# A Fourier filter and a mixture of experts on one core: zero writes and weight loads at other places, shorter row fetches, an earlier pick, an earlier flag

## The chip, the cores and the metric

The kernel runs on one core of one Trainium2 chip. The metric is the time on the device in microseconds (us), from the start of the launch to its end. The kernel before takes 481.42 us, the median of three runs (480.68 to 495.76). The profiled execution shows a span of 480.1 us; all times below that name a moment are counted from the start of this span.

## The reference

Eight sequences of 2496 tokens with 256 channels go through a filter in the frequency domain. Then each token goes to one of eight experts, an expert keeps the 80 tokens with the largest gate, and only kept tokens get a result; all others are zero.

```python
X = np.fft.rfft(x, axis=1)                      # x: 8 x 2496 x 256
y = np.fft.irfft(X * (filt_r + 1j * filt_i), n=2496, axis=1)
x = y.reshape(19968, 256)

logits = x @ w_gate                             # 8 experts
expert_idx = np.argmax(logits, axis=1)
gate_w = softmax(logits)[np.arange(N), expert_idx]
out = np.zeros((N, D))
for e in range(8):
    tok_idx = np.where(expert_idx == e)[0]
    if len(tok_idx) > 80:                       # keep the 80 largest gates
        keep = np.argpartition(-gate_w[tok_idx], 80)[:80]
        tok_idx = tok_idx[keep]
    h = np.maximum(x[tok_idx] @ w1[e], 0.0)     # 256 x 1024
    out[tok_idx] = gate_w[tok_idx, None] * (h @ w2[e])
```

At most 640 of 19,968 rows are not zero. So the kernel transforms back only the picked tokens, and writes the zeros of the output (20 MB) itself.

## The kernel before

It has three stretches.

1. **Steps** (about 24 to 292 us): 80 steps, ten for each of the eight sequences, take the spectrum, multiply it with the filter and turn it. `step(k)` also runs what a plan has put at step k: loads, logits, gating (the candidates' keys), zero writes. After the fifth sequence a first `pick` chooses places among those five.
2. **Groups** (about 298 to 400 us): 40 groups, five for each sequence, fetch for each picked token its row of a table (10 KB), turn it, and multiply it with the sequence's spectrum. Up to 128 tokens of one sequence are one tile. The result of a sequence goes to `y_sel` in device memory. `aside[i]` names what else is issued after group i: spectra (`yb`), zeros, weights, the second pick. The sequences go in the order 0, 1, 3, 4, 2, 5, 6, 7.
3. **Experts** (about 400 to 471 us): the tokens of each expert are gathered from `y_sel` (those of the last sequence come from on-chip memory through a product with a one-hot matrix), and go through the two layers; results are scattered into the output. A flag `bad` says if the quick choice was not exact; then a slow path under `tc.If` does all again. With this input it is not entered.

The parts that the change and the prediction touch, cut:

```python
def put_zeros(n):                       # 26 pieces of 768 KB, on SyncE's DMA queue
    for i in zeros[:n]:
        nc.sync.dma_start(out=out[...], in_=zero_t[...])
    del zeros[:n]

def load_weights(e, pool, tag):         # two DMAs of 1 MB, on SyncE's queue
    w = pool.tile([128, NS, C], F32, ...)
    nc.sync.dma_start(out=w1, in_=moe_w1[e]...)
    nc.sync.dma_start(out=w2, in_=moe_w2[e]...)

# end of pick(): the list of rows for each sequence; lo is -1 where a place is free
nc.vector.tensor_scalar(out=idxb[:, nb0:nb], in0=lo[:, 0:n_b], scalar1=0.0, op0=AL.max)

# plan of the steps (NU = 10 steps a sequence; "put(step, place, what)")
k = NU * 4 + LATE                       # 42
for b0, at0 in ((0, 5), (2, 11)):       # keys of sequences 0,1 and 2,3
    for i, at in enumerate((0, 0, 1, 2, 4, 5)):
        put(k + at0 + at, 2, part(gating, b0, i))
k = NU * NA + LATE                      # 52
put(k + 2, 1, part(logits, 4, 4, 0, 0))
for i, at in enumerate((7, 7, 8, 8, 10, 11)):
    put(k + at, 2, part(gating, 4, i))
for at in (12, 13, 14, 15, 16, 17, 19, 20, 21, 22, 24):
    put(k + at, 0, more_pick)
for at in (2, 3, 3, 4, 4, 5, 5, 6, 7, 8, 10, 12, 14, 16, 18, 20, 22, 24):
    put(NU * 4 + at, 2, part(put_zeros, 1))

def fetch(t):                           # 128 rows of 10 KB, indirect DMA from GpSimd
    gts[t] = pools["mn"[t % 2]].tile([128, NS * 128], F32, ...)
    nc.gpsimd.indirect_dma_start(out=gts[t][:], in_=rows[:, :], in_offset=...idxb[:, b:b + 1])

# the groups
def turn_rows(i):                       # 4 transposes, ScalarE copies; then fetch(t + 2)
    ...
def rows_out(i):                        # 4 products of the token tile with the spectrum
    ...
    if g == NGR - 1:
        nc.scalar.copy(out=yr[:], in_=po)
        if t + 1 < B:
            nc.sync.dma_start(out=y_sel[128 * b:128 * b + 128, :], in_=yr[:])
        else:
            st["yr"] = yr

def gather_slots():                     # issued after group 35
    for e in range(E):
        nc.gpsimd.indirect_dma_start(out=xg[:, e, :], in_=y_sel[:, :], in_offset=...idx1[:, e:e + 1])

for e, i in enumerate((30, 35, 26, 37, 39)):
    aside[i].append(part(load_weights, e, ...))
for i in (2, 4, 5, 24, 27, 29, 31, 33):
    aside[i].append(lambda: put_zeros(1))
for i in range(B * NGR + 1):
    if i < B * NGR: turn_rows(i)
    if i: rows_out(i - 1)
    for f in aside.get(i, ()): f()

# the experts
slots_in(0); slots_last(0); slots_in(1); slots_last(1)   # px: turn the gathered tokens
hT = layer1(0, ...)
for e in range(E):
    if e + 1 < E: hT2 = layer1(e + 1, ...)
    layer2(e, hT, ...)                  # ends in the scatter of expert e
    hT = hT2
    if e + 5 < E: load_weights(e + 5, ...)

n_bad = nc.values_load(bad[0:1, 0:1], min_val=0, max_val=1 << 20)
with tc.If(n_bad > 0), ExitStack() as ictx:
    ...                                 # slow path, not entered
```

Of the kernel before, what the change touches and what calls it, by code (L numbers as in the profile page):

```python
# [90 lines left out]
def kernel(  # L91
# [146 lines left out]
    with ExitStack() as fctx, tc.manual_schedule():  # L238
# [329 lines left out]
        def pick(final):  # L568
# [146 lines left out]
            for k in range(KR):  # L715
# [6 lines left out]
                                           in1=lo[:, 0:n_b], op0=AL.mult, op1=AL.add)  # L722
            nc.vector.tensor_scalar(out=idxb[:, nb0:nb], in0=lo[:, 0:n_b], scalar1=0.0,
                                    scalar2=None, op0=AL.max)

# [161 lines left out]
        def part(f, *a):  # L887
            return lambda: f(*a)
# [22 lines left out]
        for b, at in ((0, 3), (1, 4), (2, 6), (3, 7)):  # L911
            put(k + at, 1, part(logits, b, 0, 0, b % 2))
            put(k + at, 2, part(logits, b, 0, 1, b % 2))
        for b0, at0 in ((0, 5), (2, 11)):
            for i, at in enumerate((0, 0, 1, 2, 4, 5)):
                put(k + at0 + at, 2, part(gating, b0, i))

        k = NU * NA + LATE
        put(k, 2, part(logits_e, 4, 0))
        put(k + 2, 1, part(logits, 4, 4, 0, 0))  # L920
        put(k + 2, 2, part(logits, 4, 4, 1, 0))
        for i, at in enumerate((7, 7, 8, 8, 10, 11)):
            put(k + at, 2, part(gating, 4, i))
        for at in (12, 13, 14, 15, 16, 17, 19, 20, 21, 22, 24):
            put(k + at, 0, more_pick)
        for at in (2, 3, 3, 4, 4, 5, 5, 6, 7, 8, 10, 12, 14, 16, 18, 20, 22, 24):
            put(NU * 4 + at, 2, part(put_zeros, 1))

        gts, wts, pos = {}, {}, {}

        def fetch(t):
            b = ORDER[t]
            gts[t] = pools["mn"[t % 2]].tile([128, NS * 128], F32, name=f"gt_{b}", tag="gt")
            nc.gpsimd.indirect_dma_start(  # L934
                out=gts[t][:], out_offset=None, in_=rows[:, :],
                in_offset=bass.IndirectOffsetOnAxis(ap=idxb[:, b:b + 1], axis=0))

# [5 lines left out]

        put(k + 24, 1, make_room)
        put(k + 24, 1, part(fetch, 0))

# [42 lines left out]
        def rows_out(i):  # L989
            t, g = divmod(i, NGR)  # L990
            b = ORDER[t]
            if g == 0:
                pos[t] = yps.tile([128, 2, 512], F32, name=f"po_{t}", tag="y")
            po = pos[t][:, 0, 0:C]
            for m in range(SG):
                s = SG * g + m
                nc.tensor.matmul(po, lhsT=wts[i][:, m, :], rhs=yk[b][g][:, m, :],  # L997
                                 start=(s == 0), stop=(s == NS - 1))
            if g == NGR - 1:
                yr = pools["n"].tile([128, C], F32, name=f"yr_{t}", tag="yr")  # L1000
                nc.scalar.copy(out=yr[:], in_=po)
                if t + 1 < B:
                    nc.sync.dma_start(out=y_sel[128 * b:128 * b + 128, :], in_=yr[:])
                else:
                    st["yr"] = yr

# [79 lines left out]
        for i, b in ((1, 3), (6, 4), (15, 5), (20, 6)):  # L1086
            aside.setdefault(i, []).append(part(spectrum, b))
        for e, i in enumerate((30, 35, 26, 37, 39)):
            aside.setdefault(i, []).append(part(
                load_weights, e, *((keep_b, "kb") if e < 2 else (keep_a, "ka"))))  # L1090
        for i in (2, 4, 5, 24, 27, 29, 31, 33):
            aside.setdefault(i, []).append(lambda: put_zeros(1))
# [15 lines left out]
        for e in range(E):  # L1108
            if e + 1 < E:
                hT2 = layer1(e + 1, st["xs"][:, :, e + 1, :], pools["f"])  # L1110
            layer2(e, hT, pools["f"])
            hT = hT2
# [37 lines left out]

    n_bad = nc.values_load(bad[0:1, 0:1], min_val=0, max_val=1 << 20)  # L1151
    with tc.If(n_bad > 0), ExitStack() as ictx:

# [453 lines left out]
```

## Time and profile before

| | before |
|---|---|
| time, median of three | 481.42 us |
| span of the profiled execution | 480.1 us |
| TensorE matmul busy | 440.9 us (92%) |
| VectorE / ScalarE / GpSimd busy | 183.0 / 168.7 / 155.3 us |
| bytes moved by DMA | 133.16 MB, mean 277 GB/s |
| mean granted TensorE clock | 0.96 |

The page gives for each engine the busy time, then the span in 40 slices of 12 us: each digit is the busy share of a slice in tenths. The row PEclk is the share of its full clock that TensorE was granted; the row DMA is the busy share of the 16 DMA engines. The timeline lists instructions in order of time: start, duration, engine, line of the kernel, operation, output and inputs, and in brackets how long the engine had been idle and what ended that. PE is TensorE, DVE VectorE, ACT ScalarE, POOL GpSimd, SP SyncE; a q marks what an engine's sequencer does.

### The profile page before, as it was taken

To read this page: it belongs to the slowest core of one execution; us is meant where nothing else is said; L and a number is where in the kernel's file an instruction comes from. 1 tells how busy PE (TensorE), PEld (TensorE's weight loads), DVE (VectorE), ACT (ScalarE), POOL (GpSimd) and SP (SyncE) were. 2 spreads that over 40 slices of the span, in tenths; PEclk is the share of its full clock that TensorE was granted. 3 is DMA by queue.
4 is the path that set the end of the run, shared out by engine and by line. 5 is a ranking of instruction groups with operands and counts; after the bars stand their busy time and mean duration, and the time that the engine had idled before them with its cause. 6 is when DMAs were issued, how large, how long until landed. Compare 5 with 4: busy or idle time off the path is not lost. (4 is left out here: it accounts for less than half of the span.)

```text
span 480.1 us, 7888 instructions
## 1 busy us (share of the span) xinstructions
PE 440.9 (92%) x2933; PEld 374.6 (78%) x2933; DVE 183.0 (38%) x374; ACT 168.7 (35%) x406; POOL 155.3 (32%) x219
## 2 busy tenths in 40 slices
PE   4899989899999999989999789999998997999992
PEld 4899666568788778779989788678887786988881
DVE  2376333225444344255799972242541010100000
ACT  1323534444444543552544323554321230111110
POOL 5023222225455443333566474000036005001101
PEclk9999999999999999989999989999999898799996
DMA  6869899978999999999999509497889999459200
GB/s 222 241 193 274 254 331 338 364 255 263 362 287 328 371 400 398 359 299 342 317 381 387 221 1 374 149 294 313 288 323 390 346 354 351 133 165 298 99 8 20
DMA packets 69440, 133.16 MB, mean 277 GB/s; under 512 B 5452, under 2 KB 51766, under 8 KB 67728
## 3 DMA queue, kind: packets, MB, share of 16 engines
q1 hardware_dynamic: 58838, 91.92, 57.6%
q10 hardware_dynamic: 8074, 28.27, 14.9%
q0 software_dynamic: 2480, 12.37, 7.2%
q8 instruction: 25, 0.41, 0.3%
q14 instruction: 23, 0.19, 0.1%
HBM read 81.56 MB, written 51.07 MB: 276 GB/s over the span
## 5 line engine op out<-in xcount | busy, mean ns | idle before, releaser
L409 DVE TENSOR_TENSOR p<-pb,ft 128x1024 f32<-128x1024 f32 x80 | 97.6, 1222 | 91.5 <-PE pb L404 85.4
L415 POOL TENSOR_TENSOR yt<-p 128x256 f32<-128x256 f32 x80 | 60.2, 753 | 168.0 <-PE py L427 108.2
L427 PEld LDWEIGHTS py<-gi,yt 128*128 128x128 f32 x640 | 83.4, 193 | 21.0 <-issue 11.0
L427 PE MATMUL py<-gi,yt 128*128 128x136 f32 x640 | 90.0, 284 | 6.1 <-POOL yt L417 5.7
L404 PE MATMUL pb<-d_t,t 128*128 128x128 f32 x640 | 89.3, 284 | 2.0 <-ACT t L350 1.9
L404 PEld LDWEIGHTS pb<-d_t,t 128*128 128x128 f32 x640 | 81.5, 199 | 4.6 <-ACT t L350 2.2
L348 PE MATMUL pa<-x,wf_t 128*128 128x512 f32 x128 | 61.1, 605 | 1.8 <-DMA x<-in_x_dram 1.3
L417 POOL TENSOR_TENSOR yt<-p 128x256 f32<-128x256 f32 x80 | 59.1, 739 | 0.0
L350 ACT COPY t<-pa 128x512 f32<-128x512 f32 x64 | 36.7, 587 | 53.5 <-PE pa L348 30.6
L997 PE MATMUL po<-yb,wt 128*128 128x256 f32 x160 | 39.4, 391 | 2.9 <-ACT wt L985 2.9
L985 ACT COPY wt<-pw 128x512 f32<-128x512 f32 x40 | 23.2, 586 | 49.0 <-PE pw L984 43.3
L997 PE MATMUL po<-yk,wt 128*128 128x256 f32 x160 | 37.9, 381 | 1.3 <-ACT wt L985 1.3
L348 PEld LDWEIGHTS pa<-x,wf_t 128*128 128x128 f32 x128 | 22.6, 195 | 20.9 <-issue 16.6
L450 ACT COPY ysp<-py 128x512 f32<-128x512 f32 x40 | 23.4, 585 | 39.8 <-PE py L427 22.5
L450 ACT COPY yk<-py 128x512 f32<-128x512 f32 x40 | 23.5, 587 | 33.3 <-PE py L427 30.2
L997 PEld LDWEIGHTS po<-yb,wt 128*128 128x128 f32 x160 | 29.6, 195 | 6.6 <-ACT wt L985 3.2
L997 PEld LDWEIGHTS po<-yk,wt 128*128 128x128 f32 x160 | 28.9, 190 | 4.9 <-ACT wt L985 1.8
L369 PE MATMUL pn<-wn_t,x 117*128 117x120 f32 x176 | 23.7, 295 | 8.3 <-DMA x<-in_x_dram 8.3
L1053 PEld LDWEIGHTS ph<-xs,w 128*128 128x128 f32 x256 | 30.0, 193 | 0.9 <-issue 0.4
L1053 PE MATMUL ph<-xs,w 128*128 128x80 f32 x256 | 29.6, 275 | 0.0
L369 PEld LDWEIGHTS pn<-wn_t,x 117*128 117x128 f32 x176 | 22.7, 210 | 8.6 <-issue 8.6
L934 POOL DMA_INDIRECT gt<-rows_tbl,idxb x8 | 8.7, 1081 | 62.5 <-PE pw L984 49.9
(184 smaller groups left out, 411.5 us busy)
## 6 DMA issues: line engine op xcount, KB each, us to landing
out_dram<-zero_t SPq DMA_DIRECT2D x26, 768.0 KB
x<-in_x_dram SPq DMA_DIRECT2D x32, 512.0 KB
d<-t ACTq DMA_DIRECT2D x32, 512.0 KB
w<-in_moe_w_dram SPq DMA_DIRECT2D x16, 1024.0 KB
t<-d SPq DMA_DIRECT2D x30, 512.0 KB
yf<-ysp ACTq DMA_DIRECT2D x20, 512.0 KB
yb<-yf SPq DMA_DIRECT2D x4, 2560.0 KB
x<-in_x_dram SPq DMA_DIRECT2D x25, 156.0 KB
```

The lines of the kernel that those rows point to most:

```text
L348: nc.tensor.matmul(out=ps, lhsT=wf_t, rhs=xt[:, 2 * i:2 * i + 2, :], start=True, stop=True)
L350: nc.scalar.copy(out=t1[:, 2 * i:2 * i + 2, :], in_=ps)
L369: nc.tensor.matmul(out=ps[:, j].rearrange("p h s r -> p (h s r)"), lhsT=xt[0:NP1, j, 128 * cb:128 * cb + 128], rhs=wn_t, start=True, stop= ...
L404: nc.tensor.matmul(out=ps[:, i, cb], rhs=d_t[:, s, :], start=True, stop=True, lhsT=st["t2", b, s // SG][:, s % SG, 128 * cb:128 * cb + 128])
L409: nc.vector.tensor_tensor(out=pt, in0=ps[:].rearrange("p s c r q -> p (s c) r q").unsqueeze(1).to_broadcast(shape), in1=ft[:, u].unsqueeze ...
L415: nc.gpsimd.tensor_tensor(out=yt[:, :, 0, :], in0=pt[:, 0, :, 0, :], in1=pt[:, 1, :, 1, :], op=AL.subtract)
L417: nc.gpsimd.tensor_tensor(out=yt[:, :, 1, :], in0=pt[:, 0, :, 1, :], in1=pt[:, 1, :, 0, :], op=AL.add)
L427: nc.tensor.matmul(out=ps[:, i, 136 * cb:136 * cb + 136], rhs=gi[:, cb, :], lhsT=yt[:, 2 * i + cb].rearrange("p r q -> p (r q)"), start=Tr ...
L450: nc.scalar.copy(out=ys[:, m:m + 2, :].rearrange("p i (k c) -> p i k c", k=NDB), in_=ps[:, :, 0:288].rearrange("p i (k c) -> p i k c", k=N ...
L985: nc.scalar.copy(out=wts[i][:], in_=ps[:])
L997: nc.tensor.matmul(po, lhsT=wts[i][:, m, :], rhs=yk[b][g][:, m, :], start=(s == 0), stop=(s == NS - 1))
L1053: nc.tensor.matmul(ph[:, fc // 4, fc % 4, 0:cap], lhsT=w1s[e][:, k, 128 * fc:128 * fc + 128], rhs=xs[:, k, :], start=(k == 0), stop=(k == ...
```

## The change

It has six parts.

1. **Zeros.** 15 instead of 18 of the 26 zero pieces are put in the steps, more of them between steps 62 and 72; the other 11 come after groups 2 to 27, none later. It is meant to put the writes where the DMA engines have room.
2. **Weights.** Those of experts 1, 3 and 4 are issued after the last group (40), not after 35, 37 and 39, so that they do not stand beside the gather of the tokens.
3. **Free places.** A place of a tile that no token has gets a row number beyond the table, so that a bounds check leaves it out of the fetch. The first two sequences keep row 0 in free places, so that both buffers are full once and no place holds undefined data.
4. **Keys and pick.** The keys of sequences 2 and 3 come one step sooner, those of sequence 4 and the first pick two steps sooner, and with them the first fetch.
5. **Last tile.** Its result is written to `y_sel` too, though the gather leaves it out.
6. **Flag.** `bad` is read into the engines' registers ahead of the last expert's second layer, without the check of its bounds, and the code is laid out so that the way past the slow path needs no jump.

```diff
@@ end of pick() @@
-            nc.vector.tensor_scalar(out=idxb[:, nb0:nb], in0=lo[:, 0:n_b], scalar1=0.0,
-                                    scalar2=None, op0=AL.max)
+            if not final:
+                nc.vector.tensor_scalar(out=idxb[:, 0:2], in0=lo[:, 0:2], scalar1=0.0,
+                                        scalar2=None, op0=AL.max)
+            nb1 = nb0 if final else 2
+            free = tl([128, B], F32, "free")
+            nc.vector.tensor_scalar(out=free[:, 0:nb - nb1], in0=lo[:, nb1 - nb0:n_b], scalar1=0.0,
+                                    scalar2=65536.0, op0=AL.is_lt, op1=AL.mult)
+            nc.vector.tensor_tensor(out=idxb[:, nb1:nb], in0=lo[:, nb1 - nb0:n_b],
+                                    in1=free[:, 0:nb - nb1], op=AL.add)
@@ plan of the steps @@
-        for b0, at0 in ((0, 5), (2, 11)):
-            for i, at in enumerate((0, 0, 1, 2, 4, 5)):
-                put(k + at0 + at, 2, part(gating, b0, i))
+        for b0, ats in ((0, (5, 5, 6, 7, 8, 9)), (2, (10, 10, 11, 12, 14, 15))):
+            for i, at in enumerate(ats):
+                put(k + at, 2, part(gating, b0, i))
-        put(k + 2, 1, part(logits, 4, 4, 0, 0))
+        put(k + 1, 1, part(logits, 4, 4, 0, 0))
-        for i, at in enumerate((7, 7, 8, 8, 10, 11)):
+        for i, at in enumerate((5, 5, 6, 6, 8, 9)):
             put(k + at, 2, part(gating, 4, i))
-        for at in (12, 13, 14, 15, 16, 17, 19, 20, 21, 22, 24):
+        for at in (10, 11, 12, 13, 14, 15, 17, 18, 19, 20, 22):
             put(k + at, 0, more_pick)
-        for at in (2, 3, 3, 4, 4, 5, 5, 6, 7, 8, 10, 12, 14, 16, 18, 20, 22, 24):
+        for at in (2, 3, 5, 7, 10, 14, 18, 22, 26, 27, 28, 29, 30, 31, 32):
             put(NU * 4 + at, 2, part(put_zeros, 1))
@@ fetch() @@
-                in_offset=bass.IndirectOffsetOnAxis(ap=idxb[:, b:b + 1], axis=0))
+                in_offset=bass.IndirectOffsetOnAxis(ap=idxb[:, b:b + 1], axis=0),
+                bounds_check=S - 1, oob_is_err=False)
-        put(k + 24, 1, make_room)
-        put(k + 24, 1, part(fetch, 0))
+        put(k + 22, 1, make_room)
+        put(k + 22, 1, part(fetch, 0))
@@ rows_out() @@
-                if t + 1 < B:
-                    nc.sync.dma_start(out=y_sel[128 * b:128 * b + 128, :], in_=yr[:])
-                else:
-                    st["yr"] = yr
+                nc.sync.dma_start(out=y_sel[128 * b:128 * b + 128, :], in_=yr[:])
+                st["yr"] = yr
@@ aside the groups @@
-        for e, i in enumerate((30, 35, 26, 37, 39)):
+        for e, i in ((0, 30), (1, 40), (2, 26), (3, 40), (4, 40)):
-        for i in (2, 4, 5, 24, 27, 29, 31, 33):
+        for i in (2, 3, 4, 5, 6, 13, 14, 17, 21, 24, 27):
@@ the experts @@
             if e + 1 < E:
                 hT2 = layer1(e + 1, st["xs"][:, :, e + 1, :], pools["f"])
+            else:
+                n_bad = nc.values_load(
+                    bad[0:1, 0:1], min_val=0, max_val=1 << 20,
+                    skip_runtime_bounds_check_because="a sum of counts")
             layer2(e, hT, pools["f"])
@@ the flag @@
-    n_bad = nc.values_load(bad[0:1, 0:1], min_val=0, max_val=1 << 20)
-    with tc.If(n_bad > 0), ExitStack() as ictx:
+    with tc.If(n_bad > 0, preferred_fallthrough_block=False), ExitStack() as ictx:
```

## The prediction

> **What bounds the kernel now.** I read the page's slices first, then a table of ten-microsecond stretches, then the timeline of the places where TensorE stands still, then the end.
>
> ```profile
> PE   4899989899999999989999789999998997999992
> ...
> DVE  2376333225444344255799972242541010100000
> ...
> PEclk9999999999999999989999989999999898799996
> DMA  6869899978999999999999509497889999459200
> ```
>
> TensorE is busy nearly everywhere, and DMA too, with a hole at slices 22 and 23 (264 to 288 us). A gain must come from where TensorE stands still or is slowed. The stretches name these places (columns: start and end, length, busy us and instructions of PE, PEld, DVE, ACT and POOL, granted clock, DMA share, GB/s):
>
> ```profile
> 270.00:280.00 10.00, 6.96 (x50) 6.58 (x50) 9.58 (x17) 2.20 (x7) 6.00 (x7) 0.90 0.15 59
> ...
> 360.00:370.00 10.00, 10.00 (x58) 8.76 (x57) 1.43 (x13) 2.23 (x5) 7.59 (x10) 1.00 1.00 399
> 370.00:380.00 10.00, 7.08 (x30) 5.76 (x29) 0.00 (x0) 2.43 (x5) 1.80 (x2) 0.83 1.08 390
> ...
> 390.00:400.00 10.00, 10.00 (x56) 8.77 (x53) 0.00 (x0) 2.66 (x5) 3.38 (x4) 1.00 1.07 386
> 400.00:410.00 10.00, 7.12 (x29) 5.55 (x27) 0.49 (x1) 0.80 (x2) 4.18 (x5) 0.72 1.06 331
> 410.00:420.00 10.00, 10.00 (x65) 9.21 (x65) 0.98 (x2) 0.86 (x2) 0.00 (x0) 0.77 0.31 98
> ```
>
> At 270 VectorE is full (9.58 of 10 us) and TensorE waits for it. At 360 to 380 and 390 to 410 the DMA share is 1.0 or more; TensorE drops to 7.1 us of 10, and then the clock is low too. The timeline of the second place:
>
> ```profile
> 390.34 0.34 SPq L1003 DMA_DIRECT2D y_sel<-yr  x1
> ...
> 391.76 1.89 SPq L230 DMA_DIRECT2D w<-in_moe_w_dram  x1
> ...
> 394.71 5.71 SPq L230 DMA_DIRECT2D w<-in_moe_w_dram  x1
> ...
> 395.70 0.95 POOL L1013 DMA_INDIRECT xg<-y_sel,idx  x1 [21.83 <-DMA y_sel<-yr]
> ...
> 396.68 3.62 PE L997 MATMUL po<-yk,wt 128*128 128x256 f32 x16
> ...
> 401.89 0.64 PE L1024 MATMUL px<-ident,xg 80*128 80x80 f32 x4 [1.59 <-DMA xg<-y_sel,idx]
> ...
> 404.46 0.94 POOL L1013 DMA_INDIRECT xg<-y_sel,idx  x1 [0.30 <-issue]
> ...
> 414.33 5.84 PE L1053 MATMUL ph<-xs,w 128*128 128x80 f32 x50
> ```
>
> The result of the seventh tile is sent at 390.34, but the gather waits until 395.70 for it (5.4 us). The first gathered expert is used at 401.89, 6.2 us after its issue. Between them 6 MB of weights are issued (391 to 401). TensorE has ended the groups at 400.30 (its last `po`, 396.68 + 3.62) and begins the layers at 414.33: 14.0 us for work that is short. The stretch at 360 has one more stall, 5.12 us of ScalarE with no releaser that the profile names, and TensorE stands still 2.92 us behind it:
>
> ```profile
> 372.60 1.07 ACT L985 COPY wt<-pw 128x512 f32<-128x512 f32 x2 [5.12 <-remote]
> ```
>
> The end, for GpSimd (columns: count, ns least/median/most, first and last start):
>
> ```profile
> L1152 POOLq EVENT_SEMAPHORE  x5: 17/42/43, 474.6 to 474.9; - x5
> ...
> L1152 POOLq COMPARE_BRANCH  x1: 53/53/53, 471.7 to 471.7; - x1
> ...
> L1152 POOLq INC_SWDGE_SEM  x1: 980/980/980, 475.0 to 475.0; - x1
> ```
>
> It branches at 471.7, and the next thing that its sequencer does is at 474.6, though the last scatter (issued 471.40) has its last packet at 473.6 in the trace's DMA records. From the last product (470.57) to the end (480.13) are 9.6 us.
>
> [...] the clock is 0.5 from 404.4 to 414.6[...], after the idle time at 400 to 404. [...] a gather of 80 KB takes 6.2 us beside the weights, the scatter of the same size, alone, 2.2 us (471.40 to 473.6). [...] 2.9 us from branch to next action on GpSimd, as much on VectorE (464.8 to 467.7) and ScalarE (471.2 to 474.0).
>
> **The change part by part.** I count from E, the end of the last group's products (400.30 before).
>
> *Weights after the gather (parts 2 and 5).* Nothing but the gather is then in flight from about E-13 on: the weights of expert 0 (issued 380 to 381, 2 MB at some 380 GB/s, 5.5 us) are done by then. The seventh result, issued at E-10.0, should land after about 2.3 us (the scatter's quiet time), and before it took 0.8 us from the landing to the first gather, so the gathers start at E-6.9 and not at E-4.6. They keep their spacing: eight in 8.76 us, so the last is issued at E+1.9 and lands at E+4.2. Experts 0 to 3 (16 products of 0.11 us) and their four of the last tile (1.2 us) fit between E and E+3 with no wait. After the last landing remain four products (0.45 us) and the last tile's four (1.2 us): layers from E+5.8 instead of E+14.0, so 8.2 us less. I take off 0.6 for a chance of one in three that the small gaps still halve the clock[...]. Part 5 I read as a latch: the write of the last tile must wait until the gathers have read `y_sel`, and as the weights stand behind it on SyncE's queue, they wait too. Expert 1's first megabyte is then issued near E+4.8; that of expert 5 (issued 425.23, nothing else in flight) had its last packet about 4.4 us later, so E+9.2. Layer one of expert 1 starts at E+5.8 + 3.5 (32 products of 0.11) = E+9.3. This is a tie; 0.3 us for it. Left: **7.3 us**.
>
> *Flag (part 6).* The load is 0.5 us on each sequencer, hidden: TensorE's queue runs about 3.4 us ahead there (its branch waits 3418 ns), ScalarE and GpSimd are idle. Without the jump GpSimd meets the last landing at about 473.75 and not 475.0: **1.25 us**. The 0.98 us of semaphore work and a drain of 3.26 us after it stay.
>
> *Zeros (part 1) and free places (part 3).* About 80 of 128 places are taken (640 tokens over eight sequences), so six fetches bring some 48 x 10 KB less: 2.9 MB of 133, or 7.7 us of DMA time at 380 GB/s, but each fetch had slack: that of the eighth tile was issued at 372.9 and used at 387.6. Their direct worth is nil. The zeros after groups 29, 31 and 33 (0.77 MB each, 2 us) go away from the stretch at 360 to 380, where 4.6 us are lost: 2.9 of idle time[...]. If a full DMA is the cause, this goes; if not, not. I give it 0.4 of 4.6: **1.8 us**. The zeros at steps 66 to 72 go into the hole of DMA, 256 to 275 us. The eight zero pieces that held SyncE's queue from 168 to 195 become five; TensorE has no idle time there.
>
> *Keys and pick (part 4).* It moves the full VectorE, and does not thin it: some 17 us of pick against 0.6 us of room in each step (1.82 us a step, 1.22 for the filter product). Sequence 4's first keys now fall on the step of the last ones of 2 and 3, and `idxb` costs two more operations (0.2 to 0.4 us each). The first fetch, issued at 286.9, was in time at 297.7 anyway. I set 0, from +0.5 to -1.
>
> Sum: 7.3 + 1.25 + 1.8 = 10.4 us off, **481.4 to 471.0 us**.
>
> **The rivals.** (a) *The weights become the bound.* They start some 14 us later; if the latch lets go late or two megabytes must land first, TensorE waits 2 to 4 us ahead of layer one of expert 1: 474 to 475. For it: the tie above. Against it: only the first of the two megabytes is needed there, and later experts have 14 us more. (b) *The gather stays slow.* If the write of the last tile does not wait, the weights meet gathers five to eight, which take 6.2 us again: last landing near E+8, layers from E+9.6 or later with a half clock: 475 to 476. For it: nothing in the profile shows the latch. Against: gathers one to four are quiet even so. (c) *The gain is larger.* With the stall at 370 gone for good and less in the way of the steps at 200 to 230, 466 to 468. (d) *VectorE's crowding costs more*, as keys of three sequences touch: 1 to 2 us.
>
> **Range and chances.** From 466.5 (c) to 477 (a, b and d in part). Over 2% faster means under 471.8, which is close by my number: 0.54; within 2%: 0.44; slower: 0.02, as nothing is added on the path but the tie.
>
> **What would show it.** Right: the wait of the gather for `y_sel` ends about 3 us after the seventh result is issued; gathers are used at once; no clock of 0.72 at the start of the experts; layers begin near E+6; GpSimd's semaphore work starts within 0.2 us of the last landing. Wrong: weights issued before the last gather lands (b), TensorE idle ahead of the second expert (a), or the stall of 5 us near the sixth tile still there, which takes the 1.8 away.

## The result and the profile after

| | before | after |
|---|---|---|
| time, median (four executions of each on one chip) | 481.05 us (480.55 to 495.76) | 478.85 us (473.77 to 483.32) |
| ratio after/before, 95% interval | | 0.9864 (0.9828 to 0.9899) |
| span of the profiled execution | 480.1 us | 481.0 us |
| TensorE matmul busy | 440.9 us | 438.5 us |
| bytes moved by DMA | 133.16 MB | 131.20 MB |
| mean granted TensorE clock of that execution | 0.960 | 0.963 |

The change makes the kernel 1.4% faster, where 2.2% (481.4 to 471.0 us) was predicted. The medians here are of all executions, the ratios only of those within 1.5% of the fastest of the same kernel, so 0.9864 is not 478.85 / 481.05. By the ratio the kernel after stands at 474.5 us (0.9864 x 481.05), inside the predicted range; the median of all four lies 1.85 us above that range. Measured a second time, unchanged (after_again below), the ratio was 0.995: the two measurements put the gain at 0.5 and 1.4%. Executions of one and the same kernel differ by up to 3.7% (before, in the set of after_again), and the clock that TensorE was granted differs with them: after_again took 474.91 us at a mean clock of 0.977 and 488.62 us at 0.949. So most of what follows counts from E, the end of the last group's products, inside one execution.

Slices of the page of after, in the order of those of before:

```profile
PE   4889989799999999989989699989999799899990
...
DVE  2466323135444344355699972143532010000000
...
PEclk9999989999999999987999999999999999599996
DMA  6768889987999998297689988199999943989000
```

The hole of DMA at slices 22 and 23 is full (9 and 8): that is where the zeros of steps 66 to 72 (issued up to 273.8) and the first fetch (283.6, before 286.9) went; lower ones now stand at slices 16 (2) and 25 (1, before 4). The loss of clock at the start of the experts is not gone: PEclk shows a 5 at slice 34, where before it showed 8 and 7 at slices 33 and 34. The same stretches as before (columns: start and end, length, busy us and instructions of PE, PEld, DVE, ACT and POOL, granted clock, DMA share, GB/s):

```profile
360.00:370.00 10.00, 10.00 (x59) 8.72 (x58) 2.54 (x16) 2.71 (x5) 6.45 (x8) 1.00 0.99 372
370.00:380.00 10.00, 6.98 (x39) 5.97 (x38) 0.00 (x0) 2.03 (x4) 3.33 (x4) 1.00 1.00 349
390.00:400.00 10.00, 10.00 (x56) 8.82 (x55) 0.00 (x0) 2.71 (x5) 5.12 (x6) 1.00 0.15 46
400.00:410.00 10.00, 10.00 (x76) 9.17 (x74) 0.98 (x2) 1.22 (x3) 2.44 (x3) 1.00 0.50 159
410.00:420.00 10.00, 8.48 (x37) 7.93 (x37) 0.98 (x2) 0.87 (x2) 0.00 (x0) 0.56 1.07 383
```

From 390 to 400 DMA is nearly empty (0.15, before 1.07), and TensorE works through from 390 to 410 (before 7.12 of the second ten). At 370 it still loses 3 us, as before. At 410 there is a new loss: 8.48 us busy and a clock of 0.56. The timeline around E = 400.77 (start, duration, engine, line, operation, output and inputs, and in brackets the idle time and what ended it):

```profile
390.82 14.31 SPq L1012 DMA_DIRECT2D y_sel<-yr  x2
...
393.35 0.95 POOL L1021 DMA_INDIRECT xg<-y_sel,idx  x1 [17.28 <-DMA y_sel<-yr]
...
397.15 3.62 PE L1007 MATMUL po<-yk,wt 128*128 128x256 f32 x16
...
400.61 1.91 PE L1032 MATMUL px<-ident,xg 80*128 80x80 f32 x16
...
402.11 0.95 POOL L1021 DMA_INDIRECT xg<-y_sel,idx  x1 [0.30 <-issue]
...
405.23 0.38 SPq L230 DMA_DIRECT2D w<-in_moe_w_dram  x1
...
406.34 3.69 PE L1061 MATMUL ph<-xs,w 128*128 128x80 f32 x32
...
411.56 0.72 PE L1061 MATMUL ph<-xs,w 128*128 128x80 f32 x2 [1.52 <-DMA w<-in_moe_w_dram]
```

The seventh result is sent at 390.82, and the first gather starts 2.5 us later (before 5.4). All gathered experts are used without a wait. The second instruction of the first line is the write of the last tile; it is issued only at about 405, after the last gather (issued 402.11) has landed, and the weights stand behind it (405.23). The layers begin at 406.34 = E+5.57, before E+14.04. But 3.7 us later (406.34 + 3.69), at expert 1, TensorE waits 1.52 us for the weights, and the trace's clock records then show 0.5 from 411.2 for 10.2 us.

The stall beside the sixth tile is there as before, to within 0.1 us (5.12 of ScalarE and 2.92 of TensorE before):

```profile
374.75 1.07 ACT L995 COPY wt<-pw 128x512 f32<-128x512 f32 x2 [5.14 <-remote]
...
375.39 1.99 PE L1007 MATMUL po<-yb,wt 128*128 128x256 f32 x8 [3.02 <-ACT wt L995]
```

And the end, the line of `tc.If` for GpSimd (count, ns least/median/most, first and last start):

```profile
L1163 POOLq EVENT_SEMAPHORE  x5: 17/42/43, 469.6 to 472.6; - x5
...
L1163 POOLq COMPARE_BRANCH  x2: 40/40/41, 469.5 to 473.7; - x2
...
L1163 POOLq INC_SWDGE_SEM  x1: 972/972/972, 472.7 to 472.7; - x1
```

There are two branches now. The first, at 469.5, costs nothing: the next record is 0.09 us later. The second stands at 473.7, behind the semaphore work. GpSimd's own records, after and before, show what comes behind it (start, ns, operation; cut):

```
after                              before
469.543   40 COMPARE_BRANCH        471.401  906 DMA_INDIRECT (last scatter)
469.776  909 DMA_INDIRECT (last)   471.749   53 COMPARE_BRANCH
...                                ...
472.526   42 EVENT_SEMAPHORE       474.601   17 EVENT_SEMAPHORE
472.699  972 INC_SWDGE_SEM         475.017  980 INC_SWDGE_SEM
473.707   41 COMPARE_BRANCH         ...
476.354 3330 DRAIN                 476.028 3255 DRAIN
```

Before, 2.85 us pass behind the branch at 471.749, partly beside the flight of the last scatter. After, 2.65 us pass behind the branch at 473.707, beside nothing. From the last product to the end are 12.06 us, before 9.56.

### The profile page after: what moved, and what is told of

Read it like the earlier page. It is cut to its first block, busy times and chain, and to the rows that moved or that the text cites. A ratio compares the mean times of both kernels' runs of the same rounds, so it can differ in the third digit from the quotient of the medians.

```text
span 481.0 us, 7904 instructions
## 1 busy us (share of the span) xinstructions
PE 438.5 (91%) x2933; PEld 373.0 (78%) x2933; DVE 182.4 (38%) x377; ACT 169.0 (35%) x406; POOL 155.5 (32%) x219
## 2 busy tenths in 40 slices
DMA packets 69583, 131.20 MB, mean 273 GB/s; under 512 B 5671, under 2 KB 52113, under 8 KB 68075
## 3 DMA queue, kind: packets, MB, share of 16 engines
q0 software_dynamic: 2480, 10.30, 5.9%
## 5 line engine op out<-in xcount | busy, mean ns | idle before, releaser
L427 PEld LDWEIGHTS py<-gi,yt 128*128 128x128 f32 x640 | 82.4, 191 | 22.4 <-POOL yt L417 11.2
L427 PE MATMUL py<-gi,yt 128*128 128x136 f32 x640 | 88.7, 282 | 7.4 <-POOL yt L417 7.4
L404 PE MATMUL pb<-d_t,t 128*128 128x128 f32 x640 | 87.8, 281 | 2.7 <-ACT t L350 2.1
L404 PEld LDWEIGHTS pb<-d_t,t 128*128 128x128 f32 x640 | 79.9, 195 | 5.3 <-ACT t L350 2.3
L1007 PE MATMUL po<-yb,wt 128*128 128x256 f32 x160 | 37.9, 380 | 3.0 <-ACT wt L995 3.0
L1061 PEld LDWEIGHTS ph<-xs,w 128*128 128x128 f32 x256 | 33.0, 209 | 2.4 <-DMA w<-in_moe_w_dram 1.7
L1061 PE MATMUL ph<-xs,w 128*128 128x80 f32 x256 | 33.0, 292 | 1.5 <-DMA w<-in_moe_w_dram 1.5
L369 PEld LDWEIGHTS pn<-wn_t,x 117*128 117x128 f32 x176 | 22.8, 210 | 10.3 <-issue 8.9
L1075 PE MATMUL pe<-w,hT 128*80 128x256 f32 x128 | 30.3, 393 | 0.0
```

Of the source, the lines that this page charges most:

```text
L369: nc.tensor.matmul(out=ps[:, j].rearrange("p h s r -> p (h s r)"), lhsT=xt[0:NP1, j, 128 * cb:128 * cb + 128], rhs=wn_t, start=True, stop= ...
L404: nc.tensor.matmul(out=ps[:, i, cb], rhs=d_t[:, s, :], start=True, stop=True, lhsT=st["t2", b, s // SG][:, s % SG, 128 * cb:128 * cb + 128])
L427: nc.tensor.matmul(out=ps[:, i, 136 * cb:136 * cb + 136], rhs=gi[:, cb, :], lhsT=yt[:, 2 * i + cb].rearrange("p r q -> p (r q)"), start=Tr ...
L1061: nc.tensor.matmul(ph[:, fc // 4, fc % 4, 0:cap], lhsT=w1s[e][:, k, 128 * fc:128 * fc + 128], rhs=xs[:, k, :], start=(k == 0), stop=(k == ...
L1075: nc.tensor.matmul(po[0:cap, :], lhsT=hT[:, fc, :], rhs=w2s[e][:, fc, :], start=(fc == 0), stop=(fc == NFC - 1))
```

## The experiments

My theory after these readings: the gain at the start of the experts is as large as predicted, and is given back at two places which the change itself makes, the wait for expert 1's weights (with the half clock behind it) and the jump that the new layout has put at the very end. The rivals: that reading the flag early is what costs at the end, that the earlier pick or the crowded steps eat the gain, or that part 5 does nothing and the program place of the weights alone brings what is seen. A third question is the stall beside the sixth tile.

The table puts all profiled executions side by side, in us: the layers' start, expert 1's layer and the last product, counted from E; how long the clock was halved behind the layers' start; the end counted from the last product (tail) and from E. The last column is an estimate of where E would stand at full clock: E less half of the time at half clock before it.

| kernel | layers | expert 1 | last product | halved | tail | E to end | E at full clock |
|---|---|---|---|---|---|---|---|
| before | 14.04 | 17.71 | 70.27 | 0.3 | 9.56 | 79.83 | 390.1 |
| after | 5.57 | 10.79 | 68.17 | 10.2 | 12.06 | 80.23 | 392.2 |
| after_again | 5.57 | 10.96 | 66.86 | 6.8 | 11.77 | 78.63 | 393.3 |
| flag_at_end | 5.57 | 10.87 | 66.77 | 6.8 | 10.25 | 77.03 | 393.2 |
| flag_early_old_layout | 5.61 | 11.08 | 63.71 | 0 | 9.64 | 73.36 | 390.5 |
| w1_after_35 | 5.70 | 9.23 | 61.80 | 0 | 12.10 | 73.89 | 394.2 |
| before_plus_weights | 7.89 | 12.49 | 65.12 | 0 | 9.85 | 74.97 | 391.4 |
| no_latch | 10.23 | 14.53 | 67.09 | 1.6 | 12.11 | 79.20 | 392.0 |
| old_layout_w1_35 | 5.57 | 9.10 | 61.67 | 0 | 9.59 | 71.26 | 392.7 |
| gates_after_29 | 5.57 | 9.10 | 61.67 | 0 | 9.61 | 71.27 | 390.7 |
| gates_after_29b | 5.71 | 9.24 | 61.80 | 0 | 9.37 | 71.17 | 390.8 |
| pick_old | 5.64 | 9.17 | 61.74 | 0 | 9.29 | 71.03 | 391.7 |
| zeros_old | 7.21 | 10.74 | 63.31 | 0 | 9.22 | 72.53 | 391.9 |
| w2_after_32 | 11.64 | 15.77 | 68.34 | 1.2 | 9.44 | 77.78 | 389.9 |

Where I write "at equal clock", a straight line was put through the times of all executions of all kernels against the mean clock of each: 468 us for 1.0 of clock, with one constant for each kernel, read at a clock of 0.970. It is within 1.4 us (standard deviation). It gives before 479.9 to 480.9 +-0.7 in three sets of executions, and after 478.6 to 478.9. It counts a half clock as a loss even where the gathers set the pace, as before at E+4 to E+14 (the last gather lands at 410.80, E+10.5), so it is used only between kernels that don't differ in that.

### 1. flag_at_end: after, with part 6 undone

```diff
-            else:
-                n_bad = nc.values_load(bad[0:1, 0:1], ..., skip_runtime_bounds_check_because=...)
...
-    with tc.If(n_bad > 0, preferred_fallthrough_block=False), ExitStack() as ictx:
+    n_bad = nc.values_load(bad[0:1, 0:1], min_val=0, max_val=1 << 20)
+    with tc.If(n_bad > 0), ExitStack() as ictx:
```

> The kernel after with part 6 undone (flag read at the end, code laid out as before). Theory: the new layout does not take the jump away, it moves it behind the last semaphore work of GpSimd (branch at 473.7, drain only at 476.4), where nothing hides it[...]. So the stretch from the last product to the end goes back from 12.1 us to about 9.6, and the time from about 474.3 to about 471.8. Rival (the prediction's step): the jump of before cost 1.25 us, and the long end of the kernel after is an accident of that one execution; then about 475.5.

Measured: 478.61 us (474.2 to 484.32), ratio to before 0.9951 (0.9915 to 0.9986); at equal clock 476.9 +-0.7. The tail is 10.25 us: 1.5 to 1.8 us less than in the two executions of after. So part 6 as a whole costs time. Which half of it, the next one says.

### 2. flag_early_old_layout: after, with the flag read early but the code laid out as before

```diff
-    with tc.If(n_bad > 0, preferred_fallthrough_block=False), ExitStack() as ictx:
+    with tc.If(n_bad > 0), ExitStack() as ictx:
```

> The kernel after with the early read of the flag, but the code laid out as before (the way past the slow path jumps). Theory: the branch now comes some 0.6 us sooner than in the kernel before[...]: last product to end about 8.4 to 8.8 us, 470.7 to 471.3. Rival: the early read brings nothing, only the layout counts: equal to the run with the flag at the end, about 471.8. Second rival (the prediction): the jump cannot hide, and this is slower than the kernel after by 1 us or so.

Measured: 477.28 us (469.16 to 482.81), ratio 0.9846 (0.9803 to 0.9889); at equal clock 477.4 +-0.6, the same as with the read at the end. The tail is 9.64 us. The same line of the profile, for GpSimd:

```profile
L1163 POOLq EVENT_SEMAPHORE  x5: 17/43/43, 466.4 to 466.7; - x5
...
L1163 POOLq COMPARE_BRANCH  x1: 53/53/53, 463.4 to 463.4; - x1
...
L1163 POOLq INC_SWDGE_SEM  x1: 980/980/980, 466.8 to 466.8; - x1
```

One branch again, and the 3 us behind it lie beside the last scatter. I had expected 8.4 to 8.8 us, with these 3 us hidden whole; they are not. The early read costs nothing and brings nothing that these runs could tell from zero; the layout costs 2 to 2.5 us. In the four profiled executions with the new layout the tail is 11.8 to 12.1 us, in the ten others 9.2 to 10.3.

### 3. w1_after_35: after, with expert 1's weights issued after group 35 again

```diff
-        for e, i in ((0, 30), (1, 40), (2, 26), (3, 40), (4, 40)):
+        for e, i in ((0, 30), (1, 35), (2, 26), (3, 40), (4, 40)):
```

> The kernel after with the weights of expert 1 issued after group 35 again, those of 3 and 4 still after group 40. Theory: the wait of 1.5 us ahead of the second expert goes, and with it the half clock of 10 us that follows in the profile of the kernel after; the gather stays quiet, since 2 MB are in by about 397. Experts still begin about 5.6 us after the last group. 472.8 if only the wait goes, down to 469 with the clock, and the runs of this kernel spread less than those of the kernel after (473.8 to 483.3). Rival: two megabytes ahead of the gathers delay the seventh result and the first gathers by 2 to 3 us, experts begin at 8 us after the last group, no gain: 474 or more. Second rival: the half clock comes from the small products of the gather and not from the wait, then it stays, and only 1.5 us go.

Measured: 474.06 us (467.55 to 478.58), ratio 0.9776 (0.9717 to 0.9834). The timeline behind E = 402.75:

```profile
408.45 6.82 PE L1061 MATMUL ph<-xs,w 128*128 128x80 f32 x60
```

The wait ahead of expert 1 is gone (E+9.23 is E+5.70 and the 32 products), the clock is not halved, and the last product comes at E+61.80, 6.4 us sooner than in after and 5.1 sooner than in after_again. The 2 MB stand ahead of the gathers and do slow the first of them: by the trace's semaphore records it lands 5.8 us after its issue, in after 2.3. But that is still 1.6 us before E, and the last gather, issued when the 2 MB have landed, takes 2.6 us (2.3 in after), so the layers begin at E+5.70. So the loss at expert 1 is the weights' lateness, and it was the larger of the two.

### 4. before_plus_weights: the kernel before, with parts 2 and 5 alone

```diff
-                if t + 1 < B:
-                    nc.sync.dma_start(out=y_sel[128 * b:128 * b + 128, :], in_=yr[:])
-                else:
-                    st["yr"] = yr
+                nc.sync.dma_start(out=y_sel[128 * b:128 * b + 128, :], in_=yr[:])
+                st["yr"] = yr
...
-        for e, i in enumerate((30, 35, 26, 37, 39)):
+        for e, i in ((0, 30), (1, 40), (2, 26), (3, 40), (4, 40)):
```

> The kernel before with parts 2 and 5 alone (weights of experts 1, 3 and 4 after the last group, last tile written to y_sel). Theory: this is nearly all of the gain: experts begin 5.6 us after the last group instead of 14.0, less 1.5 us of wait for the weights of expert 1, clock as before: 480.6 - 8.4 + 1.5 = 473.7, so no slower than the whole change. Rival: zeros, free places and the earlier pick carry a part, in that the gather is only quiet without the late zeros: 476 or more.

Measured: 479.79 us (474.59 to 490.09), ratio 0.9954 (0.9927 to 0.9982). The layers begin at E+7.89: 6.2 us of the 8.5, not all. The rest is the first gather, which is late as before (E-5.07):

```profile
389.94 16.73 SPq L1002 DMA_DIRECT2D y_sel<-yr  x2
...
394.82 0.95 POOL L1011 DMA_INDIRECT xg<-y_sel,idx  x1 [21.36 <-DMA y_sel<-yr]
...
412.39 2.79 PE L1051 MATMUL ph<-xs,w 128*128 128x80 f32 x23 [0.91 <-DMA w<-in_moe_w_dram]
```

The seventh result takes 4.9 us to the first gather, not 2.5, though no weights follow it. What is in its way must have been issued before it. Run 9 says what. The layers are later than in after by what the first gather is later (2.32 and 2.35 us).

### 5. after_again: the kernel after, unchanged

> The kernel after as it is, beside the next three on one chip. Theory: experts begin 5.6 us after the last group, expert 1 waits 1.5 to 1.8 us for its weights, last product to end 12.1 us; the time follows the granted clock at some 450 us for each 1.0 of it, and is about 478.9 at a clock of 0.970. Rival: the first four runs met an unlucky chip, and on this one the time is 474 without a higher clock.

Measured: 478.95 us (474.91 to 488.62), ratio 0.995 (0.9907 to 0.9992). It repeats the readings of after: layers at E+5.57, a wait of 1.70 us at expert 1, half clock for 6.8 us, tail 11.77. The interval of this ratio does not touch that of the first measurement: an interval from one chip does not cover the differences in clock from one set of executions to another.

### 6. no_latch: after, with part 5 undone

```diff
-                nc.sync.dma_start(out=y_sel[128 * b:128 * b + 128, :], in_=yr[:])
-                st["yr"] = yr
+                if t + 1 < B:
+                    nc.sync.dma_start(out=y_sel[128 * b:128 * b + 128, :], in_=yr[:])
+                else:
+                    st["yr"] = yr
```

> The kernel after with part 5 undone: the last tile is not written to y_sel, the weights still stand after group 40 in the program. Theory: the place in the program alone does nothing, since SyncE's queue waits for nothing there; without the write that has to wait for the gathers, the weights are issued at about 391 right behind the seventh result, as in the kernel before, each gather takes 6 us again, and the experts begin 12 to 14 us after the last group. About 482 at a clock of 0.970. Rival (the prediction's): the weights come only after the last group, gathers one to four are quiet, experts begin at 9 to 10 us. Second rival: part 5 is without effect, 5.6 us.

Measured: 481.07 us (473.95 to 488.48), ratio 0.99 (0.98 to 0.9999). The timeline around E = 400.49:

```profile
390.54 0.34 SPq L1013 DMA_DIRECT2D y_sel<-yr  x1
...
390.97 0.39 SPq L230 DMA_DIRECT2D w<-in_moe_w_dram  x1
...
393.12 0.95 POOL L1023 DMA_INDIRECT xg<-y_sel,idx  x1 [18.99 <-DMA y_sel<-yr]
...
407.00 0.67 PE L1034 MATMUL px<-ident,xg 80*128 80x80 f32 x4 [0.85 <-DMA xg<-y_sel,idx]
...
410.73 1.62 PE L1063 MATMUL ph<-xs,w 128*128 128x80 f32 x7
```

The program issues these weights after group 40, but SyncE has nothing to wait for and sends them 0.43 us behind the seventh result, 9.5 us before E. The gathers then land late one after the other, and the layers begin at E+10.23. The write of the last tile, whose data nobody reads, is what holds the weights back: part 5 is the latch that the prediction took it for, and without it the place in the program does nothing. I had expected a start at E+12 or later, as before; the first gather is on time here (2.6 us behind the send), as no late zeros stand ahead of the seventh result (run 9); before, it was also sent ahead of the weights, and took 5.4 us.

### 7. old_layout_w1_35: edits 2 and 3 together

> The kernel after with the code laid out as before (flag still read early) and the weights of expert 1 issued after group 35. Theory: both gains add, 2.3 us at the end and 1.5 us of wait, so 475.1 at a clock of 0.970; and as no wait puts the clock down at the start of the experts, the mean clock is 0.975 or more, so that the median is 471 to 473. Rival: the higher clock of the six runs with the weights after group 35 was luck, then the median is 475 to 476.

Measured: 468.02 us (464.82 to 476.02), ratio 0.9696 (0.9635 to 0.9756), 3.0% faster than before and the lowest median here. From E to the end it takes 71.26 us, 8.57 less than before. Clock, and timeline around E = 394.40:

```profile
PEclk9999999999999999989999999999999999999997
```

```profile
384.45 0.34 SPq L1012 DMA_DIRECT2D y_sel<-yr  x1
...
384.88 0.39 SPq L230 DMA_DIRECT2D w<-in_moe_w_dram  x1
...
387.02 0.95 POOL L1021 DMA_INDIRECT xg<-y_sel,idx  x1 [17.30 <-DMA y_sel<-yr]
...
398.88 0.43 SPq L230 DMA_DIRECT2D w<-in_moe_w_dram  x1
...
399.97 6.26 PE L1061 MATMUL ph<-xs,w 128*128 128x80 f32 x55
```

Expert 1's weights leave at 384.88, those of experts 3 and 4 behind the latch at 398.88, and the layers run 55 products on end. No slice of the experts has a low clock.

### 8. gates_after_29: run 7, with the last call of the second pick after group 29

```diff
-        for i in (..., 23, 24, 25, 26):
+        for i in (..., 23, 24, 25, 29):
```

> The run before this one, with the last part of the second pick (the product pv, the flag, and the eight gathers of gates on GpSimd) after group 29 instead of 26. In all traces ScalarE stands still 4 to 5 us in group 28, and TensorE 2.9 us behind it. Theory one: this stall comes from the eight gathers of gates or from pv, and moves by three groups, to group 31. Theory two (the prediction's): it comes from DMA being full with the weights of expert 2, the seventh tile's rows and zeros, and stays in group 28 or goes. Time: no change, within 1 us at equal clock, if it only moves.

This edit moved nothing: the pick has ended in the call before, and the one moved is empty. So it is a repeat of run 7: 471.77 us (469.54 to 473.31), ratio 0.9777 (0.9713 to 0.984), E to end 71.27 us, the stall at its old place. Runs 7 and 8 together put the gain of this version at 2.2 to 3.0%.

### 9. zeros_old: run 7, with part 1 undone

```diff
-        for at in (2, 3, 5, 7, 10, 14, 18, 22, 26, 27, 28, 29, 30, 31, 32):
+        for at in (2, 3, 3, 4, 4, 5, 5, 6, 7, 8, 10, 12, 14, 16, 18, 20, 22, 24):
...
-        for i in (2, 3, 4, 5, 6, 13, 14, 17, 21, 24, 27):
+        for i in (2, 4, 5, 24, 27, 29, 31, 33):
```

> The combined kernel with part 1 undone: zero pieces at the steps and groups of the kernel before, three of them after groups 29, 31 and 33. Theory: they are in the queue ahead of the seventh result, as in the run of the kernel before with late weights, so the first gather starts at E-5 (E: end of the last group's products) instead of E-7.4, and the experts begin at E+8 instead of E+5.6: 2.3 us more at equal clock, 477.4 at 0.970. Rival: with the weights of expert 1 also ahead of the last tile's write, the delay is larger, 4 us and more. Second rival: the zeros matter nowhere, 475.1.

Measured: 477.78 us (472.28 to 488.12), ratio 0.9911 (0.987 to 0.9952); at equal clock 478.6 +-0.7, against 475.2 +-1.2 of run 7.

```profile
392.18 0.34 SPq L1012 DMA_DIRECT2D y_sel<-yr  x1
...
396.40 0.95 POOL L1021 DMA_INDIRECT xg<-y_sel,idx  x1 [19.95 <-DMA y_sel<-yr]
...
406.53 0.67 PE L1032 MATMUL px<-ident,xg 80*128 80x80 f32 x4 [0.50 <-DMA xg<-y_sel,idx]
```

With zeros after groups 29, 31 and 33 again, the seventh result takes 4.2 us instead of 2.6, TensorE waits for the last gathers, and the layers begin at E+7.21. The semaphore records show the line that forms: the last of the late zeros, issued at E-17.9, lands at E-6.8, and the seventh result, issued at E-9.95 behind it on SyncE's queue, at E-6.56; in run 7, without late zeros, it lands at E-8.22. That is 1.6 us at the first gather and at the layers; the difference at equal clock is larger (3.4 +-1.4), and what makes up the rest was not found.

### 10. pick_old: run 7, with part 4 undone

```diff
-        for b0, ats in ((0, (5, 5, 6, 7, 8, 9)), (2, (10, 10, 11, 12, 14, 15))):
+        for b0, ats in ((0, (5, 5, 6, 7, 9, 10)), (2, (11, 11, 12, 13, 15, 16))):
...
-        for at in (10, 11, 12, 13, 14, 15, 17, 18, 19, 20, 22):
+        for at in (12, 13, 14, 15, 16, 17, 19, 20, 21, 22, 24):
...
-        put(k + 22, 1, part(fetch, 0))
+        put(k + 24, 1, part(fetch, 0))
```

(Logits and keys of sequence 4 and `make_room` go back as well.)

> The combined kernel (flag early, old layout, weights of expert 1 after group 35) with part 4 undone: keys and pick two steps later, as in the kernel before. Theory (prediction's step, worth nothing): at equal clock within 1 us of the combined kernel's 475.1 at 0.970; steps 42 to 79 take as long within 1 us. Rival: the earlier pick crowds VectorE more, since the keys of sequence 4 meet those of 2 and 3, and undoing it saves 1 to 2 us (steps 52 to 79: 68.7 us in the kernel before, 66.7 to 70.9 in kernels with the earlier pick). Second rival: it saves something, and undoing costs 1 us or more.

Measured: 470.35 us (468.29 to 474.92), ratio 0.9773 (0.9665 to 0.9881); at equal clock 476.1 +-1.4 against 475.2 +-1.2 of run 7 and 474.4 +-1.4 of run 8. No difference can be told.

### 11 and 12. gates_after_29b and w2_after_32: what makes the stall beside the sixth tile?

Both start from run 7. The first moves the last two calls of the second pick, and with them the eight gathers of the gates on GpSimd's queue, behind groups 29 and 30. The second takes 2 MB of weights out of the stretch where the stall is.

```diff
-        for i in (..., 23, 24, 25, 26):          # gates_after_29b
+        for i in (..., 23, 24, 29, 30):
```
```diff
-        for e, i in ((0, 30), (1, 35), (2, 26), (3, 40), (4, 40)):    # w2_after_32
+        for e, i in ((0, 30), (1, 35), (2, 32), (3, 40), (4, 40)):
```

> The combined kernel with the last working part of the second pick (pv, flag, eight gathers of gates) after group 29; the run labelled gates_after_29 moved only an empty call. Theory one: the stall of ScalarE in group 28 (4 to 5 us, TensorE 2.9 to 3.1) comes from pv or the gathers of gates and goes from group 28, to show again some three groups after them. Theory two: it comes from the weights of expert 2 and the row fetch that fill DMA there, and stays in group 28.

> The combined kernel with the weights of expert 2 after group 32 instead of 26. Theory two (DMA full at groups 26 to 29 holds something up): the stall in group 28 goes, and TensorE has no idle time of 2.9 us there; 3 us less at equal clock, if the weights do not delay the seventh result. Theory one (pv or gates): the stall stays in group 28.

One execution of each: 472.34 and 479.75 us. gates_after_29b:

```profile
380.50 0.95 POOL L841 DMA_INDIRECT gate<-gates,idxs  x1 [0.30 <-issue]
382.49 0.59 ACT L995 COPY wt<-pw 128x512 f32<-128x512 f32 x1 [5.22 <-PE pw L994]
383.13 1.81 PEld L1007 LDWEIGHTS po<-yb,wt 128*128 128x128 f32 x8 [2.44 <-ACT wt L995]
383.13 2.53 PE L1007 MATMUL po<-yb,wt 128*128 128x256 f32 x8 [2.21 <-ACT wt L995]
```

The stall has left the sixth tile; TensorE now stands still at 381 to 383, right behind the last of the eight gathers, and ScalarE for the same 5.2 us before 382.49. The bracket names the last product (`pw`) that had ended by then, at 380.92; counted in order, the product that this copy turns over had ended at 378.76, 3.7 us before. In w2_after_32 it stays in its place:

```profile
374.14 0.58 ACT L995 COPY wt<-pw 128x512 f32<-128x512 f32 x1 [3.71 <-PE pw L994]
```

It is shorter there (3.71 us of ScalarE, 1.50 of TensorE). So the place of the stall goes with the calls that were moved. These hold the product `pv` and the flag too, but `pv` had ended at 371.77, 5.5 us before ScalarE stood still, while in all fourteen profiled executions ScalarE goes on 0.3 to 1.9 us behind the issue of the last gate gather. That speaks for the gathers; a run that moves them without `pv` was not made. What sets the stall's length is less clear, as it is shorter with 2 MB less beside it here, but also with the late zeros beside it (4.41 and 2.23 us in run 9). Why ScalarE should stand still beside eight gathers of 80 numbers each, the traces don't show; this stays open. The weights of expert 2, after group 32, meet the result of the seventh tile instead (5.75 us to the first gather, layers at E+11.64), which shows the cost of late bytes once more.

## Why the prediction was right in part

- **Layers at E+5.8 instead of E+14.0: held.** Measured E+5.57, 8.47 us sooner, for 8.2. The steps of it held too: 2.5 us from the send to the first gather (3.1 predicted), the last gather issued at E+1.3 (E+1.9), no wait for any. What failed is the split of it. The prediction gave all of it to parts 2 and 5; these alone bring 6.15 us (run 4). The other 2.3 come from the rest of the change, and part 1 is 1.6 of them (run 9).
- **The latch of part 5: held.** Nothing in the profile of before showed it; run 6 did. Rival (b), the gather slow without a latch, came to E+10.23 there, near its E+9.6.
- **"This is a tie; 0.3 us for it": failed.** It is the term that cost most. Expert 1's layer waits 1.5 to 1.8 us, since its first megabyte, issued at E+4.5, takes until E+10.7: 6.3 us, and not the 4.4 of expert 5's. The latch was not late (E+4.8 predicted); the term for the landing was too small. The 4.4 end with the last packet; by the semaphore records the sixteen parts of expert 5's megabyte are all in after 4.9 us. Of expert 1's in after, fifteen are in after 5.1 us, and the sixteenth follows 1.15 us later (expert 5's: 0.05). The five megabytes issued behind it are not the main cause: 222 of its 256 packets had ended before the first packet of the next megabyte began (409.41). The DMA records of after have one packet of 16 KB of instructions beside this transfer (409.43, 0.88 us), and those of before none beside expert 5's; that it held up the last part was not tested, and the cause stays open.
- **The 0.6 us for a half clock: too small.** It was an estimate; by the length of before's stretch at half clock at 373.65 it is a third of half of 3.41 us. Behind the wait stand 10.2 us at half clock in after and 6.8 in after_again, worth half of that; without the wait there are none (runs 3 and 7), though with it there need not be (run 2: 1.78 us of wait, none). In before, TensorE stood still for 2.10 of the 3.41 us ahead of the half clock (400.96 to 404.37). In us from E to the last product: -8.47 for the layers, +1.55 for the wait, +4.8 behind it = -2.1 in after (70.27 to 68.17); -8.47 + 1.70 + 3.3 = -3.4 in after_again. Predicted was -7.3. Without the wait it is -8.5 to -8.6 (runs 3 and 7). This is rival (a), the wait for the weights, and the half clock makes it worse than the 2 to 4 us given to it.
- **"Without the jump": failed.** The flag was to bring 1.25 us and costs 2.2 to 2.5. The start of GpSimd's semaphore work did come forward: it is 3.75 us behind the last product, before 4.45, so 0.7 (0.72 us behind the last packet of the last scatter, before 1.40; within 0.2 was predicted). But a jump is still made, 2.65 us long, behind that work, and the drain and the end behind it are 0.55 us longer: -0.7 + 2.65 + 0.55 = +2.5. Of the 0.55 us, 0.47 stand in flag_at_end and flag_early_old_layout too, so they are not the jump's. The step failed in reading "needs no jump" past the slow path as "no jump is made". In the old place 1.87 of the jump's 2.85 us lay beside the last scatter (last packet at 473.62).
- **The stall beside the sixth tile, 0.4 of 4.6 us: nil.** The 4.6 us are the 2.92 of idle time and half of the 3.41 us at half clock behind it (before, 373.65 to 377.06). Zeros were not its cause; it is in every kernel (ScalarE idle for 3.7 to 6.0 us), with the zeros back after groups 29, 31 and 33 even a little shorter than without (4.4 us in run 9, 5.2 in run 7), and it goes where the calls with the gate gathers go (run 11).
- **Zeros, direct worth nil: failed,** to the other side. I had asked whether the fetches have slack, and they do. The small write of the seventh result behind them has none.
- **Keys and pick, 0: held** within what can be measured (run 10). Nothing at all was won before E: at full clock E stands at 390.1 before and at 392.2 and 393.3 after, within the 389.9 to 394.2 of all kernels. Free places (part 3) were not tried alone; GpSimd's queue moves 10.30 MB instead of 12.37, so 2.1 MB less, where 2.9 were predicted.

The sum comes out in another kernel, but by luck. The prediction has 7.3 + 1.25 = 8.55 us from E to the end; run 7, which repairs the two failed steps with two edits, has 8.57 (79.83 to 71.26). Of these, 8.60 lie ahead of the last product, where 7.3 were predicted, and the tail brings nothing (9.56 and 9.59), where 1.25 were predicted. Its median gains more (3.0%, and 2.2% in the repeat) as its clock is higher: 0.984 on average, against 0.964 to 0.967 before. The half clock that is missing behind E is a part of that; the time at half clock before E also varies, in executions of the same code, from 3.4 to 17 us (runs 7 and 8), which no edit here accounts for.

## What to carry to other kernels

When transfers are moved behind an event, work out when the first of them is needed and what else stands on the queue beside it; keep the one needed first ahead of the event if what it slows has time to spare (in run 3, the first gather: 5.8 us to its landing instead of 2.3, and still 1.6 us ahead of E). A write that nobody needs held the queue here (the weights left at E+4.5 in after); the place in the program alone did not (E-9.5 in run 6). A layout that makes the usual way fall through has to be followed to the last instruction: here the jump at the end of the kernel stood beside nothing (tail 11.8 to 12.1 us), the one beside the last transfer was mostly hidden (9.2 to 10.3).

## What was not expected of the hardware

- The jump past the slow path took GpSimd 2.65 us to its next instruction in after and 2.85 us in before, and 2.9 to 3.1 us in flag_at_end, flag_early_old_layout and old_layout_w1_35, wherever it stood.
- A wait of 1.5 to 1.8 us of TensorE was followed by 0, 6.8, 6.8 and 10.2 us at half clock in four executions with the same wait, and in six without that wait by none (column "halved" of the table). Up to the last experts, the clock records of before show 0.5 for 3.41 us from 22.08, 93.76, 209.81, 226.88, 278.08 and 373.65, and for 10.24 us from 404.37; those of after for 3.41 us from 66.48, 209.84 and 298.59, for 6.83 us from 223.49 and for 10.24 us from 411.23. By these two traces the starts lie whole multiples of 3.41 us apart, to within 0.05 us. In the 3.41 us just ahead TensorE stood still for 2.92 us at 373.65 and 2.10 us at 404.37 (before), and for 1.19 us at 411.23 (after). Yet in after it stood still for 1.31 us from 370.27 to 373.68 and for 1.71 us from 373.68 to 377.09, and no half clock followed. How much idle time brings one, these runs do not show.
- ScalarE stood still for 3.7 to 6.0 us beside eight gathers of 80 numbers each on GpSimd's queue, though it needs nothing from them; when the calls with these gathers were moved, the stall moved.
